# Query loads of a retention-plus-MLP kernel: runs of four tokens, four heads in each half of the partitions

## The chip, the core and the metric

The kernel runs on one core of a Trainium2 chip. A core has TensorE (PE in the profile; PEld is its weight load), VectorE (DVE), ScalarE (ACT), GpSimd (POOL) and SyncE (SP, which here only issues DMAs), 16 DMA engines that they share, an on-chip memory of 128 partitions and PSUM with 8 banks, into which TensorE writes. The metric is the device time of one execution in microseconds; a kernel's time is the median of its runs.

## The reference

Eight batches, eight heads, 576 tokens, head size 64. Retention (scores times a decay that depends on the distance of the tokens, no softmax), then a two-layer MLP with g = h cos(h). All inputs and the output are float32.

```python
scores = scale * np.matmul(q, k.transpose(0, 1, 3, 2))            # q, k, v: (8, 8, 576, 64)
gamma = 1.0 - 2.0 ** (-5.0 - np.arange(H, dtype=np.float32))
Dmat = np.where(rel >= 0, gamma[:, None, None] ** rel[None, :, :], 0.0)   # rel = query pos - key pos
attn = np.matmul(scores * Dmat[None], v)
x = attn.transpose(0, 2, 1, 3).reshape(4608, 512)
h = x @ w_in                                                      # (512, 2048)
out = (h * np.cos(h)) @ w_out                                     # (2048, 512)
```

## The kernel before

**Retention.** Each batch is cut into two units of 256 tokens and a remainder of 64. Since gamma^(i-j) = gamma^i gamma^-j, q is multiplied by a table of gamma^i/8 (WQ) and v by one of gamma^-j (WV) when they are cast to bf16 (line 597: `qnat`, `natv`); k is only cast (`natk`, line 548). Inside a unit the scores are masked with 0 or 1 (`pt`, line 706, tables TR); between stretches of a unit, and between units, a state K'V is carried (`sba`, `sbb`, `sbr`). q and k are transposed to `qt` and `kt`, in the first four units by TensorE (line 621, copied out of PSUM by ScalarE or VectorE), later by DMA transposes (line 636). Scores, states and outputs are 64x64 matmuls, four side by side on the array (line 667). The outputs are copied from PSUM to `xt` as x transposed (lines 547 and 548).

**Coarse and fine.** Six units, those of batches 0 and 1 and the first of batches 2 and 3, are *coarse*: a partition holds two neighbouring tokens of all eight heads, loaded in one DMA of 512 KB in runs of 512 bytes, and stretches have 128 tokens. The other ten are *fine*: a partition holds one token, each half of 128 tokens has its own DMA in runs of 256 bytes, and stretches have 64 tokens. Remainders have one DMA of 128 KB per batch, on the lower or the upper 64 partitions.

**MLP.** Two units, one of each of two batches, form a tile of 512 tokens; there are nine. The first layer of tiles 0 to 3 is direct (lines 871, 880, 883), that of tiles 4 to 8 goes by seven products in place of eight (lines 983 to 1000), as does the second layer of all (line 1140). For tile 0 two quarters of the first layer are done for each batch by itself, so that they can begin when the first unit is through.

**What sets the order.** The kernel is built as a graph of tasks with estimated durations (lines 131 to 364). A planner runs that graph once, with one list of work for each engine, and the order that it gives is written out as the program; `SHIFT` (line 382) is a table of corrections to the tasks' priorities. Each engine then works through its list in that order and waits on semaphores. All loads of q, k and v are issued by SP in one queue, among them the transposes and the stores; the weights (`win`, `wout`) are issued by GpSimd, each behind the landing of certain q or k loads (`SLABS`, line 380). q has two staging buffers (`stgq`). Where the planner sees a gap on TensorE in the first part, it puts in matmuls on a tile of ones (`warm`, line 492); they compute nothing that is used.

The program starts with the loads that wait for nothing, then the constants (line 498 on: iota and affine_select on GpSimd, memsets on VectorE, exp on ScalarE), and then the planned order.

Of the kernel before, what the change touches and what calls it, by code (L numbers as in the profile page):

```python
# [6 lines left out]
ALU = mybir.AluOpType  # L7
AF = mybir.ActivationFunctionType
F32 = mybir.dt.float32
BF16 = mybir.dt.bfloat16  # L10
# [358 lines left out]
class Kernel:  # L369
# [13 lines left out]
        "Iic;6r$0X*%'(rv/|*2|K$-\\.xP)s7VxS/#u$F?$1t%6D&')'Zx%YG1f<&\\T$aB&y6*G5/`r,{w)zf2bt)t5)^Z,n4&w<)v3&r%"  # L383
        "%4c*\\T-a&$t#%ll%h1%ZX)kq'uX%fA$pg+h6%|)$c)8#U%k4%@E'gh(gT&u7({#&,)<q|/w,,wz%b(-v+.o6&mQ2z]'|&3zK&im"
        "'HD$3A&Dx(G@$(M&(+/#U'.$,=b&-()(`&3C&#h&#U(lF$Md/F7((E&>A$#U(|K%F++wd$cl%t6/F|'qh$sM$Rq$\\n&SH(;8'k8"
        "%q$%nx$Cu&p/$o)&vD$I+.+5.lh'X7&do%1a(8`&lN$5F$|K&xt'2Y(:k4lM0ho'|K6{y%42-4WE:n)l,$t@&|K${y(v2*6u,n/"
        "$|K$|K'z5(eg+k8&3,*Y\\%mf*.J8#U.vK,Y@7l`&l6'`,-w<+wQ(o2$|K%wF$-O%v|(/>.j4-i)%dp$om-|K24w&$7)<+*>=%\\V"
        "(HH-jx-iu**H+5a&u,$@V%i3$NR%p7)iR'j8&kV$fS&qI,0-*Pk.WA-:&+a`'6.1rc,)L-hD&ux%KK*U?'1@'Ym&K{'d5&:r%/i"
        "+pa%d^%ap$oN$(T$_G'oQ,CJ$#Y,3t$#U)vZ1|K&=S$)k$/^$3:0n5$xC&^`2%nB86''y&#x%#U=ve'R'&k3%Y2&j1'd8'xH(iL"
        '-8w'  # L390
# [9 lines left out]
    def __init__(self, nc, es, q, k, v, w_in, w_out, out):  # L400
# [10 lines left out]
        self.WV = sb("wv", [128, NT], F32)  # L411
        self.WQ = sb("wq", [128, NT], F32)
        self.IDN = sb("idn", [128, 128], BF16)
        self.TR = {2: sb("tr2", [128, 256], BF16), 1: sb("tr1", [128, 64], BF16)}
        self.TB = {2: sb("tb2", [128, 256], BF16), 1: sb("tb1", [128, 64], BF16)}
# [82 lines left out]
    def constants(self):  # L498
# [4 lines left out]
        for y in range(2):  # L503
# [5 lines left out]
            allow_small_or_imprecise_dtypes=True), w=[("i", 4)])  # L509
        for i, t in enumerate((self.IA, self.IB)):  # L510
            P.add("pool", lambda e, i=i, t=t: e.iota(
                ap(t, NT, 0, 128, 32, [1, 8]), [[0, 8]], base=512 - 64 * i, channel_multiplier=1,
                allow_small_or_imprecise_dtypes=True), w=[("i", 2 + i)])
# [3 lines left out]
        for h in range(H):  # L517
            P.add("dve", lambda e, h=h: e.memset(ap(self.LG, NT, 0, 128, h, [8, NT // 8]), lng[h]), w=[("lg", h)])
        P.add("dve", lambda e: e.memset(self.CPI.ap(), math.pi / 2), w=["cpi"])
        P.add("dve", lambda e: e.tensor_copy(ap(self.IA, NT, 64, 64, 32, [1, 8]), ap(self.IB, NT, 64, 64, 32, [1, 8])),  # L520
# [793 lines left out]
```

## Time and profile before

| | |
|---|---|
| median of 3 runs | 285.07 us (284.45 to 286.09) |
| profiled execution | 284.38 us |
| its span, from the first instruction to the last | 282.6 us |
| busy: PE, DVE, ACT, POOL | 274.2, 224.0, 175.5, 151.8 us |
| granted TensorE clock | 1.0 |
| read from and written to HBM | 36.70 MB and 9.44 MB |
| q loads: 512 KB x6, 256 KB x20, 128 KB x8; median from issue to landing | 7.1, 5.0, 3.4 us |

The page gives totals, a strip of 40 slices of the span (7.07 us each) with the busy share in tenths, the DMA queues, and the costliest groups of instructions. Besides it the trace answers questions: the chain of work that ended last (each step is what released the next), stretches of the span with the busy time of each engine, all instructions in order of time, and for a tile, who waits for it. A line in a group is the line of the kernel that issued it.

### The profile page before, as it was taken

The numbers are of one execution on the slowest core, as the hardware profiler recorded it, in microseconds if no ns is written. First come the engines' busy times: TensorE is split into PE (matmuls) and PEld (weight loads), VectorE is DVE, ScalarE is ACT, GpSimd is POOL, SyncE is SP. The second block draws the span as 40 slices with busy tenths as digits, with TensorE's granted clock in tenths as the row PEclk, the third lists the DMA queues.
The fourth block names the chain that finished last, engine by engine and source line by source line (L and its number), as shares of the span: only waits on it lengthen the run. The fifth ranks groups of instructions, "written<-read, shape, count | busy, mean of one in ns | idle before, by whom it ended". The sixth has DMA issues, their size and how long they took to land.

```text
span 282.6 us, 9717 instructions
## 1 busy us (share of the span) xinstructions
PE 274.2 (97%) x4093; PEld 216.6 (77%) x4093; DVE 224.0 (79%) x387; ACT 175.5 (62%) x357; POOL 151.8 (54%) x170
## 2 busy tenths in 40 slices
PE   7889989999999999999999999999999999999995
PEld 2457577888884667557888888888888888888884
DVE  3587789998757788888778896799769988896762
ACT  5257866372537645763567767895784777787420
POOL 5461942478244625744789659966495161545300
PEclk9999999999999999999999999999999999999999
DMA  7999999999999999999999999997861200400115
GB/s 197 266 224 278 251 186 265 285 208 219 199 229 204 175 235 175 244 178 250 286 170 224 241 206 235 198 201 171 176 77 69 81 6 0 151 0 2 72 41 187
DMA packets 133131, 49.91 MB, mean 177 GB/s; under 512 B 105440, under 2 KB 128992, under 8 KB 133088
## 3 DMA queue, kind: packets, MB, share of 16 engines
q1 hardware_dynamic: 128576, 44.84, 75.0%
q0 software_dynamic: 4224, 4.19, 9.3%
q8 instruction: 32, 0.52, 0.8%
q10 hardware_dynamic: 288, 0.26, 0.3%
q14 instruction: 11, 0.09, 0.1%
HBM read 36.70 MB, written 9.44 MB: 163 GB/s over the span
## 4 chain that ended last, share of the span: by engine, by line
PE 93%; DVE 3%; DMA 1%; ACT 1%; issue 0%; DVEq 0%
PE bk L1140 40%; PE bk L1000 22%; PE bk L871 19%; PE bk L667 10%; DVE pt L706 2%; DMA stgq<-in_q_dram 1%; PE bk L621 1%; PE bk L492 1%; ACT cb L880 1%; DVE gt L883 0%; DVE kt L548 0%; DVE qnat L597 0%; ACT xt L547 0%; ACT natk L547 0%; ACT qt L547 0%
## 5 line engine op out<-in xcount | busy, mean ns | idle before, releaser
L989 POOL TENSOR_TENSOR gt<-sq,cb 128x512 bf16<-128x512 f32 x40 | 45.9, 1161 | 35.5 <-ACT cb L985 13.1
L871 PE MATMUL bk<-xt,win 128*128 128x256 bf16 (+1 forms) x352 | 60.7, 321 | 0.7 <-ACT xt L547 0.5
L880 ACT ACTIVATE cb<-bk 128x256 bf16<-128x256 f32 (+1 forms) x88 | 41.9, 483 | 21.3 <-PE bk L871 19.0
L883 DVE TENSOR_TENSOR gt<-bk,cb 128x256 bf16<-128x256 f32 (+1 forms) x88 | 46.3, 542 | 10.9 <-ACT cb L880 7.9
L597 POOL TENSOR_TENSOR natv<-stgv,wv 128x512 bf16<-128x512 f32 x36 | 37.2, 1042 | 31.6 <-DVE s L1077 8.2
L871 PEld LDWEIGHTS bk<-xt,win 128*128 128x128 bf16 x352 | 33.1, 98 | 20.2 <-ACT xt L547 1.3
L597 POOL TENSOR_TENSOR qnat<-stgq,wq 128x512 bf16<-128x512 f32 x32 | 33.3, 1049 | 27.5 <-DMA stgq<-in_q_dram 8.9
L989 DVE TENSOR_TENSOR gt<-bk,cb 128x512 bf16<-128x512 f32 x40 | 27.1, 687 | 11.5 <-ACT cb L985 10.8
L1140 PE MATMUL bk<-wout,s 128*128 128x256 bf16 x288 | 36.3, 273 | 0.0
L1140 PE MATMUL bk<-tw,s 128*128 128x256 bf16 x288 | 36.2, 273 | 0.0
L1140 PE MATMUL bk<-wout,gt 128*128 128x256 bf16 x288 | 35.7, 273 | 0.0
L1000 PE MATMUL bk<-xt,win 128*128 128x256 bf16 x240 | 34.7, 273 | 0.0
L706 DVE TENSOR_TENSOR pt<-bk,tr 128x512 bf16<-128x512 f32 x48 | 30.6, 683 | 3.0 <-PE bk L667 3.0
L547 ACT ACTIVATE sn<-bk 128x512 f32<-128x512 f32 (+1 forms) x29 | 16.2, 567 | 26.8 <-PE bk L1140 26.7
L983 DVE TENSOR_TENSOR sq<-bk,sq 128x512 f32<-128x512 f32 x40 | 27.0, 685 | 5.8 <-PE bk L1000 4.9
L1140 PEld LDWEIGHTS bk<-tw,s 128*128 128x128 bf16 x288 | 27.6, 98 | 4.1
L1140 PEld LDWEIGHTS bk<-wout,s 128*128 128x128 bf16 x288 | 27.6, 98 | 3.9
L1140 PEld LDWEIGHTS bk<-wout,gt 128*128 128x128 bf16 x288 | 27.9, 98 | 3.5 <-issue 0.2
L985 ACT ACTIVATE cb<-sq 128x512 bf16<-128x512 f32 x40 | 24.9, 629 | 8.7 <-DVE sq L983 7.7
L1129 DVE TENSOR_TENSOR os<-bk,sn 128x512 f32<-128x512 f32 (+1 forms) x28 | 18.6, 668 | 10.8 <-PE bk L1140 10.7
L548 POOL CAST natk<-stgk 128x512 bf16<-128x512 f32 x34 | 20.5, 622 | 9.8 <-PE bk L667 3.9
L985 ACT ACTIVATE cb<-bk 128x512 bf16<-128x512 f32 x40 | 23.5, 597 | 3.7 <-PE bk L1000 2.4
(82 smaller groups left out, 426.2 us busy)
## 6 DMA issues: line engine op xcount, KB each, us to landing
out_dram<-os SPq DMA_DIRECT2D x16, 512.0 KB, 4.1
stgk<-in_k_dram SPq DMA_DIRECT2D x20, 256.0 KB, 5.0
stgq<-in_q_dram SPq DMA_DIRECT2D x20, 256.0 KB, 5.0
stgv<-in_v_dram SPq DMA_DIRECT2D x20, 256.0 KB, 5.1
stgq<-in_q_dram SPq DMA_DIRECT2D x6, 512.0 KB, 7.1
stgk<-in_k_dram SPq DMA_DIRECT2D x6, 512.0 KB, 8.5
stgv<-in_v_dram SPq DMA_DIRECT2D x6, 512.0 KB, 8.1
win<-in_moe_w_in_dram POOLq DMA_DIRECT2D x4, 512.0 KB, 8.4
```

What stands on the lines that cost most here:

```text
L548: return self.one(eng, dur, lambda e: e.tensor_copy(dst(), src()), r=r, w=w, port=eng == "pool", **kw)
L597: self.one(eng, 610 if eng == "dve" else 1030, lambda e, out=out, inp=inp, tab=tab, col=col, hs=hs: e.tensor_tensor(out(), inp(), ap(tab, ...
L667: return lambda e: e.matmul(out(), lhs(), rhs(), start=start, stop=True, skip_group_check=True)
L706: self.one("dve", 610, lambda e, r=r, b=b, pt=pt: e.tensor_tensor(ap(self.at(pt), 1024, 0, 128, 512 * r, [64 * ny * ny, 8 // ny // ny], [1 ...
L871: inst = e.matmul(ap(self.at(bk), 512, 0, 128, 0, [1, n]), ap(self.WIN, 4 * DFF, 0, 128, c * DFF + 128 * f, [1, 128]), ap(self.at(xt), 204 ...
L880: self.one("act", n - 15, lambda e: e.activation(ap(self.at(cb), TB, 0, 128, 0, [1, n]), ap(self.at(bk), 512, 0, 128, 0, [1, n]), AF.Sin, ...
L883: self.one("dve", 75 + n / 0.96, lambda e: e.tensor_tensor(ap(self.at(gt), NF * TB, 0, 128, f * TB + 256 * h0, [1, n]), ap(self.at(bk), 51 ...
L983: self.one("dve", 610, lambda e: e.tensor_tensor(half(src), self.at(bank).ap(), half(src), ALU.add), r=[(bank,)], w=four(src))
L985: self.one("act", 530 if name else 490, lambda e: e.activation(self.at(cb).ap(), ap(self.at(src), size, 0, 128, 0, [1, 512]), AF.Sin, bias ...
L989: self.one(eng, 1120 if name else 610, lambda e: e.tensor_tensor(ap(self.at(gt), NF * TB, 0, 128, (8 * n + 2 * g) * TB + 256 * h, [TB, 2], ...
L1000: inst = e.matmul(ap(self.at(bank), 512, 0, 128, 256 * f, [1, 256]), l(c, f), rr(c), stop=True, skip_group_check=True, start=(first and f ...
L1140: inst = e.matmul(place(bank, tt), l(f, tt), rr(f), stop=True, skip_group_check=True, start=(first and f == 0 and tt < len(bank)))
```

## The change

A unit's q is loaded so that a partition holds four neighbouring tokens of four heads: heads 0 to 3 in partitions 0 to 63, heads 4 to 7 in partitions 64 to 127. That makes runs of 1 KB, and two DMAs of 256 KB for every unit, coarse or fine. The remainders stay as they are, and so do k and v. What follows from it: q has its own decay table (`WQ`, 40 columns: 8 for the remainders, 32 for the units, from the new `IQ` and `LQ`); `WV` goes into the tile `IA`. A block of `qt` then holds one of the four token residues, and `queries` picks the columns for a stretch: four runs of 32 (coarse) or 16 (fine). The masks have the queries in that order (`TR[2]` and the new `TR[4]`), and the copies to `xt` put the tokens back: they write every fourth element. In the graph a q load of a unit is two tasks with an estimate of 725 ns each on the DMA engines (before: 1840 for a coarse unit, 1200 for each half of a fine one). `SHIFT` is a new table.

```diff
--- before.py
+++ after.py
@@ -380,14 +380,13 @@
     SHIFT = (
...
     )
@@ -408,11 +407,12 @@
         self.TX = {n: sb(f"tx{n}", [128, 2048], BF16) for n in (1, 2, 4)}
-        self.WV = sb("wv", [128, NT], F32)
-        self.WQ = sb("wq", [128, NT], F32)
+        self.WQ = sb("wq", [128, 40], F32)
+        self.LQ = sb("lq", [128, 32], F32)
+        self.IQ = sb("iq", [128, 32], F32)
         self.IDN = sb("idn", [128, 128], BF16)
-        self.TR = {2: sb("tr2", [128, 256], BF16), 1: sb("tr1", [128, 64], BF16)}
-        self.TB = {2: sb("tb2", [128, 256], BF16), 1: sb("tb1", [128, 64], BF16)}
+        self.TR = {2: sb("tr2", [128, 256], BF16), 1: sb("tr1", [128, 64], BF16), 4: sb("tr4", [128, 64], BF16)}
+        self.TB = {2: sb("tb2", [128, 256], BF16), 1: sb("tb1", [128, 64], BF16), 4: sb("tb4", [128, 64], BF16)}
         self.ONE = sb("one", [128, 128], BF16)
@@ -507,6 +507,10 @@
             allow_small_or_imprecise_dtypes=True), w=[("i", 4)])
+        for i, t in enumerate((self.IQ, self.LQ)):
+            P.add("pool", lambda e, i=i, t=t: e.iota(
+                ap(t, 32, 0, 128, 0, [16, 2], [4, 4], [1, 4]), [[256, 2], [1, 4], [0, 4]], base=-256 * i, channel_multiplier=4,
+                allow_small_or_imprecise_dtypes=True), w=[("iq", i)])
         for i, t in enumerate((self.IA, self.IB)):
@@ -517,26 +521,35 @@
         P.add("dve", lambda e: e.memset(self.CPI.ap(), math.pi / 2), w=["cpi"])
+        P.add("dve", lambda e: e.tensor_copy(ap(self.IQ, 32, 64, 64, 0, [1, 32]), ap(self.LQ, 32, 64, 64, 0, [1, 32])),
+              r=[("iq", 1)], w=[("iq", 0)])
+        for h in range(H):
+            P.add("dve", lambda e, h=h: e.memset(ap(self.LQ, 32, 64 * (h // 4), 64, h % 4, [4, 8]), lng[h]),
+                  r=[("iq", 0)], w=[("iq", 1)] if h == 0 else [("lq", h)])
+        P.add("dve", lambda e: e.tensor_tensor(self.LQ.ap(), self.IQ.ap(), self.LQ.ap(), ALU.mult),
+              r=[("iq", 0), ("iq", 1)] + [("lq", h) for h in range(1, H)], w=["lqx"])
         P.add("dve", lambda e: e.tensor_copy(ap(self.IA, NT, 64, 64, 32, [1, 8]), ap(self.IB, NT, 64, 64, 32, [1, 8])),
...
               r=[("i", n) for n in (0, 1, 2, 4)] + [("lg", h) for h in range(H)], w=["lgx"])
-        P.add("act", lambda e: e.activation(self.WQ.ap(), self.LG.ap(), AF.Exp, bias=math.log(1.0 / 8.0), scale=1.0),
-              r=["lgx"], w=["wq"])
-        P.add("act", lambda e: e.activation(self.WV.ap(), self.LG.ap(), AF.Exp, scale=-1.0), r=["lgx"], w=["wv"])
+        P.add("act", lambda e: e.activation(ap(self.WQ, 40, 0, 128, 8, [1, 32]), self.LQ.ap(), AF.Exp, bias=math.log(1.0 / 8.0), scale=1.0),
+              r=["lqx"], w=["wq"])
+        P.add("act", lambda e: e.activation(ap(self.WQ, 40, 0, 128, 0, [1, 8]), ap(self.LG, NT, 0, 128, 32, [1, 8]), AF.Exp,
+                                            bias=math.log(1.0 / 8.0), scale=1.0), r=["lgx", "wq"], w=["wr"])
+        P.add("act", lambda e: e.activation(self.IA.ap(), self.LG.ap(), AF.Exp, scale=-1.0), r=["lgx"], w=["wv"])
         P.add("act", lambda e: e.activation(ap(self.IB, NT, 0, 128, 0, [1, 1]), self.CPI.ap(), AF.Sin), r=["cpi"], w=[("i", 3)])
-        for ny in (2, 1):
+        for kind, ny, run in ((2, 2, 32), (4, 1, 16), (1, 1, 64)):
             n = 64 * ny * ny
-            for dst, up, name in ((self.TR[ny], 0, "tr"), (self.TB[ny], 1, "tb")):
+            for dst, up, name in ((self.TR[kind], 0, "tr"), (self.TB[kind], 1, "tb")):
                 for y in range(ny):
-                    dims = ([64, 2], [1, 64]) if ny == 2 else ([1, 64],)
-                    P.add("pool", lambda e, dst=dst, up=up, ny=ny, y=y, n=n, dims=dims: e.affine_select(
+                    dims = ([1, 64],) if kind == 1 else ([run, 4], [1, run])
+                    P.add("pool", lambda e, dst=dst, up=up, kind=kind, ny=ny, run=run, y=y, n=n, dims=dims: e.affine_select(
                         ap(dst, n, 0, 128, 128 * y, *dims), ap(self.ONE, 128, 0, 128, 0, *dims),
-                        pattern=[[1, 2], [2, 64]] if ny == 2 else [[1, 64]], compare_op=ALU.is_ge, fill=0.0,
-                        base=64 * ny * up - y, channel_multiplier=-ny), r=["one"], w=[(name, ny, y)])
-            P.add("dve", lambda e, ny=ny, n=n: e.tensor_copy(
-                ap(self.TR[ny], n, 64, 64, 0, [1, n]), ap(self.TB[ny], n, 64, 64, 0, [1, n])),
-                r=[("tb", ny, y) for y in range(ny)], w=[("tr", ny, y) for y in range(ny)])
+                        pattern=[[1, 64]] if kind == 1 else [[1, 4], [4, run]], compare_op=ALU.is_ge, fill=0.0,
+                        base=64 * ny * up - y, channel_multiplier=-ny), r=["one"], w=[(name, kind, y)])
+            P.add("dve", lambda e, kind=kind, n=n: e.tensor_copy(
+                ap(self.TR[kind], n, 64, 64, 0, [1, n]), ap(self.TB[kind], n, 64, 64, 0, [1, n])),
+                r=[("tb", kind, y) for y in range(ny)], w=[("tr", kind, y) for y in range(ny)])
 
@@ -552,6 +565,14 @@
         src = self.src["qkv".index(which)]
+        if which == "q" and u[1] < 2:
+            for i in range(2):
+                at = (u[0] * H * S + 4 * S * i + 256 * u[1]) * D
+                self.one("sp", 500, lambda e, i=i, at=at: e.dma_start(
+                    ap(self.at(stg), 1024, 64 * i, 64, 0, [256, 4], [1, 256]),
+                    bass.AP(src, at, [[4 * D, 64], [S * D, 4], [1, 4 * D]])),
+                    r=gate, w=[(stg, i), (stg, i + 2)], sem=lambda i=i: f"{which}{stg.slot}_{i}", dma=725, tail=720 if fast else 1800)
+            return stg
         for i, (p0, n, o, ny, b, r0) in enumerate(rows):
@@ -575,10 +596,17 @@
             for y in range(2):
-                rs = [(stg, i) for i in ((2 * y, 2 * y + 1) if fine else range(4))]
+                four = which == "q" and not rem
+                rs = [(stg, i) for i in ((2 * y, 2 * y + 1) if fine and not four else range(4))]
 
...
                     return ap(self.at(nb), 1024, 0, 128, 512 * y, [256, 2], [64, 4], [1, D])
+
+                def out4(y=y, nb=nb):
+                    return ap(self.at(nb), 1024, 0, 128, 512 * y, [128, 4], [64, 2], [1, D])
+
+                def inp4(y=y, stg=stg):
+                    return ap(self.at(stg), 1024, 0, 128, 256 * y, [64, 4], [512, 2], [1, D])
 
@@ -590,12 +618,17 @@
                 else:
-                    tab, key = (self.WV, "wv") if which == "v" else (self.WQ, "wq")
+                    tab, key = (self.IA, "wv") if which == "v" else (self.WQ, "wr" if rem else "wq")
                     col = 32 if rem else 40 * fine + 16 * u[1] + 8 * y
+                    if four:
+                        out, inp, hs, col = out4, inp4, [[4, 4], [2, 2]], 8 + 16 * u[1] + y
+                    elif which == "q":
+                        col = 0
+                    nt = 40 if which == "q" else NT
                     eng = "dve" if fast and which == "q" else self.CASTS.get(u, "pp pp pp")[(3 if which == "q" else 6) + y]
                     eng = {"d": "dve", "p": "pool"}.get(eng, eng)
-                    self.one(eng, 610 if eng == "dve" else 1030, lambda e, out=out, inp=inp, tab=tab, col=col, hs=hs: e.tensor_tensor(
-                        out(), inp(), ap(tab, NT, 0, 128, col, *hs, [0, D]), ALU.mult),
+                    self.one(eng, 610 if eng == "dve" else 1030, lambda e, out=out, inp=inp, tab=tab, col=col, hs=hs, nt=nt: e.tensor_tensor(
+                        out(), inp(), ap(tab, nt, 0, 128, col, *hs, [0, D]), ALU.mult),
                         r=rs + [(key,)], w=[(nb, y)], port=eng == "pool")
@@ -666,11 +699,18 @@
 
+    def queries(self, u, qt, r, s, c, y):
+        if u[1] == 2:
+            return ap(self.at(qt), 1024, 64 * r, 64, c * 128 + 64 * s + 512 * y, [1, 64])
+        n = 16 if self.fine(u) else 32
+        return ap(self.at(qt), 1024, 64 * r, 64, 512 * (c // 2) + 64 * (c % 2) + n * (2 * y + s if n == 16 else s), [128, 4], [1, n])
+
     def scores(self, u, prio, todo, split, extra=(), join=None):
...
         N, ny = (64, 1) if rem else (128, 2)
+        kind = 4 if self.fine(u) else ny
         phases = []
@@ -681,9 +721,7 @@
                         def rhs(r=r, s=s, c=c, y=y):
-                            o = c * 128 + 64 * s
-                            return ap(self.at(qt), 1024, 64 * r, 64, o + 512 * y, [1, 64]) if rem else ap(
-                                self.at(qt), 1024, 64 * r, 64, o, [512, 2], [1, 64])
+                            return self.queries(u, qt, r, s, c, y)
                         lanes[r, s].append((N, self.mm(
@@ -706,8 +744,8 @@
                 ap(self.at(b), 512, 0, 128, 0, [64 * ny * ny, 8 // ny // ny], [1, 64 * ny * ny]),
-                ap(self.TR[ny], 64 * ny * ny, 0, 128, 0, [0, 8 // ny // ny], [1, 64 * ny * ny]), ALU.mult),
-                r=[(b,)] + [("tr", ny, y) for y in range(ny)], w=[(pt, r)])
+                ap(self.TR[kind], 64 * ny * ny, 0, 128, 0, [0, 8 // ny // ny], [1, 64 * ny * ny]), ALU.mult),
+                r=[(b,)] + [("tr", kind, y) for y in range(ny)], w=[(pt, r)])
         for v, s in todo:
@@ -771,7 +809,7 @@
                     main[s, p].append((N, self.mm(
-                        lambda c=c, y=y: ap(self.at(ob[s]), 512, 64 * p, 64, ((y * 4 if rem else 0) + c) * N, [1, N]),
+                        lambda c=c, y=y: ap(self.at(ob[s]), 512, 64 * p, 64, (2 * c + y if fine else y * 4 + c if rem else c) * N, [1, N]),
                         lambda c=c, y=y: ap(self.at(nv), 1024, 64 * s, 64, 512 * y + (2 * c + p) * D, [1, D]),
@@ -791,11 +829,9 @@
                     def rhs(i=i, y=y):
-                        o = i * 128 + 64 * s
-                        return ap(self.at(qt), 1024, 64 * r, 64, o + 512 * y, [1, 64]) if rem else ap(
-                            self.at(qt), 1024, 64 * r, 64, o, [512, 2], [1, 64])
+                        return self.queries(u, qt, r, s, i, y)
                     to[r, p].append((N, self.mm(
-                        lambda c=c, y=y: ap(self.at(ob[s]), 512, 64 * p, 64, (y * 4 + c) * N, [1, N]),
+                        lambda c=c, y=y: ap(self.at(ob[s]), 512, 64 * p, 64, (2 * c + y if fine else y * 4 + c) * N, [1, N]),
                         lambda i=i, src=src: ap(self.at(src), 256, 64 * r, 64, i * 64, [1, 64]),
@@ -814,13 +850,15 @@
             for s in range(2):
-                if rem:
-                    o, d = (64 * s, 1) if fine else (s, 2)
-                    dst = lambda o=o, d=d: ap(self.at(xt), 2048, 0, 128, 1024 * half + o, [128, 2], [256, 4], [d, 64])
+                if fine:
+                    dst = lambda s=s: ap(self.at(xt), 2048, 0, 128, 1024 * half + 64 * s, [128, 8], [1, 4], [4, 16])
+                    src = lambda s=s: ap(self.at(ob[s]), 512, 0, 128, 0, [64, 8], [16, 4], [1, 16])
+                elif rem:
+                    dst = lambda s=s: ap(self.at(xt), 2048, 0, 128, 1024 * half + s, [128, 2], [256, 4], [2, 64])
                     src = lambda s=s: ap(self.at(ob[s]), 512, 0, 128, 0, [256, 2], [64, 4], [1, 64])
                 else:
-                    dst = lambda s=s: ap(self.at(xt), 2048, 0, 128, 1024 * half + 128 * s, [256, 4], [1, 2], [2, 64])
-                    src = lambda s=s: ap(self.at(ob[s]), 512, 0, 128, 0, [128, 4], [64, 2], [1, 64])
+                    dst = lambda s=s: ap(self.at(xt), 2048, 0, 128, 1024 * half + 128 * s, [256, 4], [1, 4], [4, 32])
+                    src = lambda s=s: ap(self.at(ob[s]), 512, 0, 128, 0, [128, 4], [32, 4], [1, 32])
                 self.copy("dve" if s and (rem or u in self.SWIFT) else "act", 590, dst, src, [(ob[s],)], [(xt, half, s)])
```

More of the change, by code (lines that the diff above doesn't have):

```diff
@@ L382 @@
     SHIFT = (
[L383 to L390, printed above, removed]
+        "##h%5Q)#fBk*&|K%r7%n(X3f$^A'qx$``+J'$5/?d=/XJ,wv)vt&lJ)z/)v4&#U$&U$<($Fb$Co&#U$I99ys,#U2g^)+z)[%&|K"
+        "2_o8$=%%7$A{)zD+Cw'm\\.Gj%H$%Wx+_;&j{)no(8f&B,$K*$u/&hm$mX$%-4|K&m'&w0$mp(|C'n+'w|&\\y.{F4_g5l8)#U&?#"
+        "&9x%e)$uJ%xZ%r$%q#%k]$t4%rk%v\\%o4)ix&t/'x{4ky1{:^t,&rT&s&&tf.<5)wF&mq&zg%iI8:8+sZ,dH'Hk0:'%IU(6T*#d"
+        "'cC)x=%4W%yT%Sx$eJ'ek'8E*%v')s,497+.*?E:2A'#b%*{$km)(#+kf7r.$6Y%wy)t%$m>&{n)r:(*c(sh-Sf*z{1zL*t-@xt"
+        "%9?2?[({y&xi&s&)t(+cQ0xI$\\@4dU'%t)vd+`uG1S.-l,[x'x>%|K$nu'jz5|&)qN$sZ%zy${((qn$#U&pz*uu'oH2|K(WQ$vQ"
+        ")xL%|G${N.)['5k%cB&{[2?i&<u)?f;3S&ji4|K(k')rq&q:&o2&r>&tz&p[$wg'ec0s,.k_%t>$133S<'w?.+80&N*$j)8{$Ij"
+        "(6@+[h%XX5{]'{+&dp%|K&z#<l]0p|,Yj"
     )
```

## The prediction

> **What bounds the kernel now.** I read the page's totals and slices first, then the table of stretches, then the chain of waits, then the rates of the loads.
>
> ```profile
> PE 274.2 (97%) x4093; PEld 216.6 (77%) x4093; DVE 224.0 (79%) x387; ACT 175.5 (62%) x357; POOL 151.8 (54%) x170
> ...
> PE   7889989999999999999999999999999999999995
> ...
> DMA  7999999999999999999999999997861200400115
> ...
> q1 hardware_dynamic: 128576, 44.84, 75.0%
> ```
>
> TensorE is busy all the time but for the first six slices and the last; the DMA engines are full as well, up to slice 28. Two full resources mean that the DMA time matters only where TensorE waits for it. The stretches say where (length, then PE busy with its instructions, clock, DMA share, GB/s; in the second table filler alone, line 492, matmuls on a tile of ones that the program puts in gaps):
>
> ```profile
> 0.00:50.00 50.00, 44.86 (x608) 1.00 1.11 239
> 50.00:265.00 215.00, 214.84 (x3359) 1.00 0.84 167
> 265.00:282.60 17.60, 14.50 (x133) 1.00 0.34 121
> ```
>
> ```profile
> 0.00:50.00 50.00, 10.36 (x28) 2.82 (x28) 1.00 1.11 239
> 50.00:265.00 215.00, 0.00 (x0) 0.00 (x0) 1.00 0.84 167
> ```
>
> In the first 50 us TensorE idles 50.00 - 44.86 = 5.1 us and fills 10.4 us: 15.5 us lost. From 50 to 265 us it loses 0.16 us in all. So a faster load earns something in the first 50 us alone; a slower one can cost anywhere. The chain of waits shows the start (start, length, what):
>
> ```profile
> 0.81 4.12 DMA stgq<-in_q_dram
> 5.03 0.70 DVE qnat L597
> 5.78 1.21 PE bk L621 x8
> 6.99 0.85 PE bk L492 x2
> 7.84 0.87 PE bk L621 x8
> 8.73 0.44 DVE kt L548
> 9.30 0.66 PE bk L667 x14
> 9.99 2.50 DVE pt L706 x4
> ```
>
> q is the first load; k lies behind it in the same queue (VectorE and GpSimd turn it to bf16 from 6.81 us), and the scores at 9.30 need both. Last the rates at which loads run, from stretches filled with one kind:
>
> ```profile
> 3.50:5.00 1.50, 1.50 (x4) 0.30 (x2) 0.00 (x0) 0.53 (x2) 0.00 (x0) 1.00 1.17 326
> 79.00:83.00 4.00, 4.00 (x93) 3.43 (x91) 2.08 (x4) 1.18 (x3) 0.56 (x1) 1.00 1.19 228
> 178.00:182.00 4.00, 4.00 (x54) 3.36 (x55) 2.71 (x5) 3.40 (x8) 4.00 (x6) 1.00 0.82 187
> 190.00:192.00 2.00, 2.00 (x63) 1.80 (x63) 2.00 (x5) 1.69 (x5) 1.13 (x2) 1.00 0.83 192
> ```
>
> The first is the first q (512-byte runs, 128 partitions): 326 GB/s. The second is loads in 256-byte runs over 128 partitions: 228. The last two are the loads of the 64-token remainders: 256-byte runs again, but each DMA writes 64 partitions only, alternately the lower and the upper half: 187 and 192 GB/s, with the DMA share at 0.82 where the others show 1.17 to 1.19.
>
> **The change part by part.** The sum is made against the profiled execution, 284.38 us (span 282.6 and 1.8 around it); the median of the runs shown, 285.07, is 0.69 above it.
>
> *The q loads.* Every unit of 256 tokens gets two DMAs of 256 KB, each on one half of the partitions in 1 KB runs. For six units (the coarse ones) that replaces one DMA in 512-byte runs, for ten (fine) two DMAs in 256-byte runs. No row has 1 KB runs into 64 partitions. Lower bound: the trace's records of 1 KB packets (stores at the end, all 128 partitions) have 46 to 48 ns each, so 512 x 47 / 16 = 1.50 us for a unit. Upper bound: the 64-partition rows, 524 KB / 187 GB/s = 2.80 us. A coarse unit takes 524 / 326 = 1.61 us now, a fine one 524 / 228 = 2.30. So coarse goes from 1.61 to between 1.50 and 2.80, fine from 2.30 to the same. I take 2.76 (190 GB/s): the remainder loads are nearest, being HBM loads into the same alternating halves, and the stores share only the run length.
> The row leaves open why halves are slower, a fixed cost of each DMA or the half itself, and only the first would shrink with longer runs. [...]
>
> *First unit.* q complete moves from 4.93 us by 2.76 - 1.61 = +1.15; k, v and all that hangs on them with it. Bounds -0.11 and +1.19. SP issues one DMA more ahead of k and v (0.46 us): k's packets cannot start before q's are through, so it costs nothing; if that cover went, 0.46.
>
> *Second unit.* Its q adds another 1.15, so k lands 2.3 late; now it lands at about 14.86 (GpSimd's next weight DMA waits for it there). Its casts run at 15.59 and 16.41 and its transposes at 17.26, so about 0.9 of the 2.3 is slack: 1.4 late at the scores (18.78), and at the second half of the first tile (24.00). TensorE's only other work there is eight first-half groups, and the filler shows that they do not suffice. Delay by then: +1.4 (bounds -0.1 and +2.3).
>
> *Units three and four* (scores at 35.40 and 49.96). Their loads wait behind the weight slabs, but TensorE has solid MLP work from 24.0 to 35.4, moved by the same 1.4. A further 1.15 per load eats into that cover: I take +0.3 (bounds -0.5 and +1.2).
>
> *Two later coarse and ten fine units.* 2 x 1.15 + 10 x 0.46 = +6.9 us of DMA time at most likely, -0.2 - 8.0 = -8.2 at best. Cost nothing: after 50 us TensorE waits 0.16 us in 215. If the cover goes, see the fourth rival. SP issues six DMAs more in all, at 0.4 to 0.8 us; where its queue stands behind a buffer wait, k, v and the transposes behind it move too, which belongs to that rival.
>
> *Readers of q.* Both q multiplies of a fine unit now wait for both DMAs, where each waited for its own: at most one DMA later, 1.4 us on GpSimd (54% busy), hidden. The multiplies keep 128x512 (1047 ns). GpSimd's first weight DMA waits for the first q DMA only, so it can go out earlier (bounds: a 1.2 us gain for that slab; or the slab in front of k). Taken as zero.
>
> *Constants.* GpSimd: two iotas (0.14 to 0.18) and two selects (0.23); its list ends at 3.1 and its next work is at 5.24. VectorE: eight memsets, two copies and a multiply, some 0.9 us. ScalarE: one more exp, 0.25, before the table load that ends at 3.83. The q table is ready at about 3.2 in place of 2.36, q lands at 4.93: cover 1.7 us. Cost 0; uncovered 0.9.
>
> *Output copies.* Contiguous copies to xt take 591 to 603 ns on ScalarE, those with every second element 733 to 747. Now all write every fourth. Fine ones: from 597 to between 740 and 885 (twice the step), ten on each of ScalarE and VectorE, 1.4 to 2.9 us on an engine at 62%: hidden. Coarse: 0 to +0.15, twice on the start's path: +0.1.
>
> *Matmuls.* Scores and state reads take q columns in four runs of 32 or 16 where they had two of 64 or one. A group of 32 scores with two runs takes 0.64 us and one of 32 on contiguous pt also 0.64, so runs of 64 are free. Shorter runs: 0 by that row; if a column in short runs cost double, some 600 fine matmuls, four side by side, by 27 ns, is 4 us (fifth case). Masks have the same shape.
>
> *The order.* Which instruction stands where cannot be read from the table of shifts. Zero, with -2.0 (the stall named below) and +3 as bounds.
>
> Sum: 1.4 + 0.3 + 0.1 = +1.8: 284.38 + 1.8 = 286.2 in a profile, 285.07 + 1.8 = **286.9** as a median.
>
> **The rivals.**
> *Faster: the halves run at full rate and the new order uses it.* Place: the third unit. Its q, issued at 19.68, lands at 26.86 (GpSimd idles 7.6 us for it), scores wait until 35.40 and outputs until 38.41; between 30 and 40 us TensorE loses 0.84 idle and 1.20 filler. If q and what follows are there 2 us sooner, all 2.0 are saved; 0.1 to 0.3 more at the start: 285.07 - 2.2 = 282.9. For it: the loss is real, and 1 KB packets elsewhere do run at 47 ns. Against it: a coarse unit saves 0.11 us by that row, and the 0.8 that a fine unit saves falls where TensorE does not wait. It decides from a unit in under 1.6 us.
> *Hidden.* Halves between 1.6 and 2.0 us, start later by under 0.5, the order makes it up: 285.1. For it: if only a fixed cost per DMA explains the 0.82 share, 1 KB runs dilute it.
> *TensorE starves later.* DMA is full up to 205 us; 6.9 us more of it, and an order laid out for quick q loads, make scores wait in tiles 2 to 7, say half of 6.9: 286.9 + 3.4 = 290.3 if none is caught up, 288.5 if half is. Against it: 0.16 us of waits today.
> *Short runs slow the matmuls:* 285.07 + 4 = 289.1. Against it: 64-column runs are free.
> *The change does not do what it says*, few packets with no shorter load, is my forecast itself.
>
> **How the numbers follow.** Under 0.5% (1.4 us) this kernel's runs, 284.45 to 286.09, can't be told from no change. Forecast 0.42 (own range 285.9 to 288.0; a quarter of it inside the 0.5%), faster 0.25, hidden 0.16, starving 0.12, short runs 0.05. Faster by over 0.5%: 0.25. Within: 0.16 + 0.42/4 = 0.26. Slower: 0.49. The range leaves out about a third of the faster case below 282.9 and the dearer half of the last two above 288.8: 282.9 to 288.8.
>
> **What would show it.** q complete at about 6.1 in the chain (4.9 or less: the rate was wrong); 187 to 220 GB/s in the stretch of the first q against 326; scores of the first unit at 10.4 in place of 9.30; the second half of tile 0 at about 25.4; from 50 to 265 us PE still idle under 0.5 us; ScalarE copies to xt all at 740 or more; groups of 48 fine scores still 0.51 us. Wrong if halves are not slower, or if the new order moves filler out of the first 50 us by more than 1.8 us.

## The result and the profile after

The changed kernel takes 297.6 us (median of 6 runs, 296.95 to 298.94); the kernel before took 285.97 beside it. The ratio is 1.0416, with a 95% interval from 1.0379 to 1.0454: slower by 4.2%. The forecast was 286.9 with a range up to 288.8: the right side, and far too small. The profiled execution took 298.94 us, the longest of its six. Medians and ratios below leave out a run that lies more than 1.5% above the fastest of its kernel (one each in two experiments).

The page of the changed kernel, totals, strip and load queue:

```profile
span 297.1 us, 9745 instructions
...
PE 276.7 (93%) x4089; PEld 215.5 (73%) x4089; DVE 241.0 (81%) x398; ACT 186.4 (63%) x358; POOL 157.2 (53%) x174
...
PE   5988999999799989978999999999999999999996
...
q1 hardware_dynamic: 110240, 44.84, 72.3%
```

The queue moves the same 44.84 MB in 110240 packets in place of 128576, and their time is 72.3% of a longer span, 215 us in place of 212: fewer packets, no shorter loads. TensorE's strip has holes in the middle now. The stretches of the changed kernel (length, PE, PEld, DVE, ACT, POOL busy with their instructions, clock, DMA share, GB/s):

```profile
0.00:50.00 50.00, 42.56 (x581) 27.46 (x581) 35.02 (x86) 30.88 (x64) 25.00 (x46) 0.93 1.09 212
50.00:265.00 215.00, 204.93 (x3247) 162.56 (x3245) 183.28 (x280) 141.39 (x267) 123.46 (x121) 1.00 0.85 173
```

In the first 50 us TensorE idles 7.4 us and fills 9.3, 16.7 us where 15.5 were lost before: 1.2 more, near the +1.4 of the forecast. From 50 to 265 us it idles 10.1 us where it idled 0.16. That is most of the loss: 9.9 of the 14.5 us by which the profiled span is longer, and it lies where the forecast had put nothing. Another 2.5 us is time in which TensorE is busy, 276.7 us against 274.2. What TensorE waited for in the changed kernel (total, times, longest, all in us):

```profile
PE bk L909 <- ACT xt L560: 2.8, 5, 0.8
PE bk L700 <- issue: 2.6, 2, 1.7
PE bk L654 <- ACT natk L560: 2.6, 1, 2.6
PE bk L700 <- DMA qt<-qnat: 1.6, 1, 1.6
PE bk L700 <- POOL natk L561: 1.5, 1, 1.5
```

Two kinds stand side by side: the copies to xt (4.7 us with four smaller rows that are not shown) and data that come late out of loads, casts and transposes. (`issue` means that the profile shows nothing waited for.) The copies themselves, before and after (the first two rows are of the kernel before, the last two of the changed one; ns shortest, median, longest):

```profile
L547 ACT ACTIVATE xt<-bk x21: 589/733/752, 13.9 to 230.9; 128x512 bf16<-128x512 f32 x21
L548 DVE CAST xt<-bk x15: 678/692/742, 13.8 to 231.7; 128x512 bf16<-128x512 f32 x15
```

```profile
L560 ACT ACTIVATE xt<-bk x21: 729/1309/1418, 15.5 to 245.7; 128x512 bf16<-128x512 f32 x21
L561 DVE CAST xt<-bk x15: 730/1293/1302, 15.3 to 245.6; 128x512 bf16<-128x512 f32 x15
```

They take about twice the time; the forecast had 740 to 885. The start of the changed kernel, in order of time:

```profile
7.00 0.63 ACT L560 ACTIVATE natk<-stgk 128x512 bf16<-128x512 f32 x1 [1.86 <-DMA stgk<-in_k_dram]
7.69 1.03 PE L654 MATMUL bk<-idn,natk 128*128 128x128 bf16 x8 [2.60 <-ACT natk L560]
8.06 1.29 DVE L630 TENSOR_TENSOR qnat<-stgq,wq 128x512 bf16<-128x512 f32 x2 [3.93 <-DMA stgq<-in_q_dram]
10.63 1.07 PE L700 MATMUL bk<-qt,kt 64*64 64x128 bf16 x32 [0.18 <-DVE qt L561]
```

The new order issues half of q, then k, then the other half of q: k is cast first, the second half of q is there at 8.06 (the whole of q at 5.03 before; times of the multiply that reads it). The first scores stand at 10.63 against 9.30; the forecast had 10.4.

### The profile page after: what moved, and what is told of

It reads as the page before. It is cut to its first block, busy times and chain, and to the rows that moved or that the text cites. A ratio compares the mean times of both kernels' runs of the same rounds, so it can differ in the third digit from the quotient of the medians.

```text
span 297.1 us, 9745 instructions
## 1 busy us (share of the span) xinstructions
PE 276.7 (93%) x4089; PEld 215.5 (73%) x4089; DVE 241.0 (81%) x398; ACT 186.4 (63%) x358; POOL 157.2 (53%) x174
## 3 DMA queue, kind: packets, MB, share of 16 engines
q1 hardware_dynamic: 110240, 44.84, 72.3%
## 4 chain that ended last, share of the span: by engine, by line
PE 73%; DMA 6%; DVE 5%; ACT 5%; SPq 5%; issue 3%; POOL 2%; DVEq 0%; POOLq 0%
PE bk L1178 32%; PE bk L1038 20%; PE bk L909 13%; PE bk L700 7%; DMA stgv<-in_v_dram 5%; ACT xt L560 3%; SPq L579 2%; DVE xt L561 2%; SPq L571 2%; DVE gt L921 1%; SPq L669 1%; DMA qt<-qnat 1%; POOL tx L945 1%; POOL natv L630 1%; PE bk L654 1%
## 5 line engine op out<-in xcount | busy, mean ns | idle before, releaser
L1027 POOL TENSOR_TENSOR gt<-sq,cb 128x512 bf16<-128x512 f32 x40 | 46.7, 1169 | 43.4 <-ACT cb L1023 17.1
L921 DVE TENSOR_TENSOR gt<-bk,cb 128x256 bf16<-128x256 f32 (+1 forms) x88 | 45.5, 541 | 13.6 <-ACT cb L918 11.7
L630 POOL TENSOR_TENSOR natv<-stgv,ia 128x512 bf16<-128x512 f32 x36 | 39.2, 1097 | 21.4 <-DMA stgv<-in_v_dram 11.3
L561 POOL CAST natk<-stgk 128x512 bf16<-128x512 f32 x34 | 21.6, 642 | 37.4 <-DMA stgk<-in_k_dram 33.9
L630 POOL TENSOR_TENSOR qnat<-stgq,wq 128x512 bf16<-128x512 f32 x32 | 34.5, 1090 | 12.6 <-DMA stgq<-in_q_dram 4.5
L1178 PE MATMUL bk<-wout,gt 128*128 128x256 bf16 x288 | 36.6, 273 | 1.1 <-ACT xt L560 0.6
## 6 DMA issues: line engine op xcount, KB each, us to landing
stgv<-in_v_dram SPq DMA_DIRECT2D x6, 512.0 KB, 10.1
```

The lines of the kernel that those rows point to most:

```text
L561: return self.one(eng, dur, lambda e: e.tensor_copy(dst(), src()), r=r, w=w, port=eng == "pool", **kw)
L630: self.one(eng, 610 if eng == "dve" else 1030, lambda e, out=out, inp=inp, tab=tab, col=col, hs=hs, nt=nt: e.tensor_tensor(out(), inp(), a ...
L921: self.one("dve", 75 + n / 0.96, lambda e: e.tensor_tensor(ap(self.at(gt), NF * TB, 0, 128, f * TB + 256 * h0, [1, n]), ap(self.at(bk), 51 ...
L1027: self.one(eng, 1120 if name else 610, lambda e: e.tensor_tensor(ap(self.at(gt), NF * TB, 0, 128, (8 * n + 2 * g) * TB + 256 * h, [TB, 2], ...
L1178: inst = e.matmul(place(bank, tt), l(f, tt), rr(f), stop=True, skip_group_check=True, start=(first and f == 0 and tt < len(bank)))
```

## The experiments

Three theories were set against each other: **L**, the q loads are slower; **C**, the copies to xt are slower and hold up TensorE; **O**, the new order is worse. Ratios are to the kernel before in the same call, with 95% intervals. Kernels in the order of before have the same instructions in the same places as it, but for the edit.

**1. One part alone, in the order of before.** The loads; with them both q multiplies of a fine unit wait for both of its DMAs, as in the changed kernel:

```diff
-ap(self.at(stg), 1024, p0, n, o, [w, H], [1, w]), bass.AP(src, at, [[w, n], [S * D, H], [1, w]])
+ap(self.at(stg), 1024, 64 * i, 64, 0, [256, 4], [1, 256]), bass.AP(src, at, [[4 * D, 64], [S * D, 4], [1, 4 * D]])   # i = 0, 1
```

> The kernel before, order and copies untouched, with q loaded as the changed kernel loads it, two DMAs of 64 partitions in 1 KB runs (the multiply reads the staging tile as before, so heads and tokens are mixed up: a time of the loads alone). Theory L as recorded: q complete about 1.15 us later at the start, 287 to 288.5. Rival, the loads run at the full rate of 1 KB packets (46 ns): 285 to 286. Theory C and O leave it between these two.

Measured: 294.0 us, ratio 1.030 (1.0248 to 1.0352). Theory L, well above the range given, and five times the recorded size (8.9 us against 1.8). The copies (destinations only):

```diff
-dst: [256, 4], [1, 2], [2, 64]      # coarse; fine: [128, 2], [256, 4], [1, 64]
+dst: [256, 4], [1, 4], [4, 32]      # coarse; fine: [128, 8], [1, 4], [4, 16]
```

> The kernel before, order and loads untouched, with the copies to xt writing every fourth element as the changed kernel does (the tokens in xt are then in a wrong order; nothing else changes). Theory C: 286 rises to 292 to 297, TensorE idles at the matmuls that read xt after 50 us. Theories L and O: 286 to 288, since ScalarE is busy 62% of the span and VectorE 79%.

Measured: 290.9, ratio 1.0214 (1.0152 to 1.0277), a little under the range of theory C and well over what the other two allowed. TensorE's longest wait in that kernel:

```profile
PE bk L873 <- ACT xt L547: 3.4, 5, 1.0
```

Both together:

> The kernel before, its order untouched, with both the q loads in halves and the copies to every fourth element. If loads (8.9 alone) and copies (5.8 alone) add up: 299.5 to 300.5. If they hide behind each other: 294 to 297. Against the changed kernel (297.6) it says what the new order is worth under the new loads and copies.

Measured: 297.5, ratio 1.0394 (1.0338 to 1.045). 3.0% and 2.1% alone make 3.9% together, so a good fifth of the two hides behind each other; the time lies between the two expectations. The order of before with the new loads and copies is as slow as the changed kernel (1.0416; the intervals overlap): under them the new order, with its constants, masks and q columns, neither loses nor gains anything that these runs can tell.

**How late loads cost nine microseconds.** In the loads-alone kernel the first q multiply starts at 5.57 in place of 5.03. That is not yet the loss: the scores of the second unit start at 18.98 in place of 18.78. The delay grows along a chain that was not in the forecast: k of the fourth unit releases the weight DMAs (GpSimd, line 855 of before) at 35.5 in place of 32.4; their landing releases the loads of the next units (SP, 44.1 in place of 41.9); and SP issues the transposes of those units 4.4 and 5.5 us late (before first, loads alone second; the next ones are at 67.56 and 73.02):

```profile
55.90 2.98 SPq L636 DMA_TRANSPOSE kt<-natk  x1
```

```profile
60.31 4.15 SPq L653 DMA_TRANSPOSE kt<-natk  x1
```

TensorE, working through a fixed order, then stands (PE alone, of the kernel before and of the loads alone):

```profile
50.00:100.00 50.00, 50.00 (x835) 1.00 1.10 217
```

```profile
50.00:100.00 50.00, 44.57 (x674) 0.97 1.13 213
```

5.4 us idle in that stretch; from 100 to 265 us both are busy. The idle time is three waits: 0.91 us at 51.56 for a weight slab, 1.12 at 79.27 for VectorE, and 3.40 at 94.86 for v on GpSimd. The longest, in the loads-alone kernel:

```profile
92.76 1.05 POOL L614 TENSOR_TENSOR qnat<-stgq,wq 128x512 bf16<-128x512 f32 x1 [5.78 <-DMA stgq<-in_q_dram]
93.76 1.04 POOL L614 TENSOR_TENSOR natv<-stgv,wv 128x512 bf16<-128x512 f32 x1
...
94.86 0.32 PE L684 MATMUL bk<-natv,natk 64*64 64x64 bf16 x16 [3.40 <-POOL natv L614]
```

and the same multiply in the kernel before:

```profile
83.02 1.05 POOL L597 TENSOR_TENSOR qnat<-stgq,wq 128x512 bf16<-128x512 f32 x1
```

It is the first of the two q multiplies of a fine unit. Before, it waits for its own DMA alone, which landed at 81.89. Here it waits for both: the unit's first DMA landed at 86.88, the second, issued at 87.12 (82.96 before), at 92.69; and v stands behind it on GpSimd. No run has the halves without this wait.

Of the 9.3 us by which this span is longer, 5.5 are idle time after 50 us and 1.1 before. In the other 2.7 TensorE is busy with the same instructions: in the 5 us after the long wait its granted clock was 0.66, and the 160 first-layer matmuls of 512 columns took 38.6 us in place of 36.9. The first layer's work that fills the gaps later is not free to be moved forward, since the order is written out.

**2. What is slow in the loads.** Same order, same two DMAs of 256 KB in 1 KB runs, over all 128 partitions:

```diff
-ap(self.at(stg), 1024, 64 * i, 64, 0, [256, 4], [1, 256])
+ap(self.at(stg), 1024, 0, 128, 512 * i, [256, 2], [1, 256])
```

> As the kernel before with the q loads in halves (that one took 294.0 against 285.1), same order, same two DMAs of 256 KB in 1 KB runs, but each writes all 128 partitions (two runs in each; the bytes come from other places of q, so this is a time of the loads alone). Theory H (a DMA into 64 partitions is slow, by ports or in another way): the loss goes, 284.5 to 286.5. Rival S (two DMAs in place of one, later completion and the second multiply's wait cost it, whatever the partitions): 291 to 294.

Measured: 285.6, ratio 1.002 (0.9984 to 1.0057): the whole loss is gone, though the multiplies wait for both DMAs here too (the one above for 3.34 us, and TensorE behind it for 0.96). The halves with the old run lengths:

```diff
-ap(self.at(stg), 1024, 64 * i, 64, 0, [256, 4], [1, 256])
+ap(self.at(stg), 1024, 64 * i, 64, 0, [w, n], [1, w])    # fine: w = 64, n = 16; coarse: w = 128, n = 8
```

> The same with DMAs of 64 partitions and the old run lengths (512 and 256 bytes; bytes again from other places of q): the halves without the longer runs. Theory H: 293 or more, and at least as slow as with 1 KB runs. Rival R (1 KB runs are themselves slow into this staging tile, or collide with the 512-byte runs of k and v): 285 to 288.

Measured: 297.9, ratio 1.0439 (1.0347 to 1.053). So it is the halves; longer runs seem to soften it, but the interval just touches that of the loads alone. The queue of the two kernels with 1 KB runs, halves first:

```profile
q1 hardware_dynamic: 110240, 44.84, 75.2%
```

```profile
q1 hardware_dynamic: 110240, 44.84, 67.5%
```

The same packets, and 7.7 points less of the engines' time when they go to all partitions. In the packet records the 1 KB loads have 44 ns at the shortest in both, and a mean of 68 in halves against 55; the 512-byte packets of k and v, which did not change, have 36 against 29.

**3. Undoing parts in the changed kernel.** Copies in the old form, with the new loads and order:

```diff
-dst: [128, 8], [1, 4], [4, 16]; src: [64, 8], [16, 4], [1, 16]     # fine
+dst: [128, 8], [1, 64]; src: [64, 8], [1, 64]
```

> The changed kernel, with the copies to xt writing as the kernel before does (fine: contiguous, coarse: every second element); the tokens in xt are then in another order, so this leaves out the part of the computation that puts them back. Instruction order and loads stay as in the changed kernel. Theory C (the copies carry the loss: they take 1.29 to 1.31 us in place of 0.59 to 0.75, and lie between outputs and MLP): 297.6 falls to 287 to 290. Theory L (the slower q loads carry it, as my prediction had it): 296 to 297.5. Theory O (the new order carries it): 295 to 297.5. Copies to xt should show 590 to 750 ns on both engines.

Measured: 295.9, ratio 1.0378 (1.0326 to 1.0431). Theory C alone falls here: 1.7 us of 11.6, and the intervals of the two ratios overlap. Loads in the old form, with the slow copies:

```diff
-ap(self.at(stg), 1024, 64 * i, 64, 0, [256, 4], [1, 256])
+ap(self.at(stg), 1024, 0, 128, 512 * i, [w, hs], [1, w])     # fine: w = 64, hs = 8; coarse: w = 128, hs = 4
```

> The changed kernel with only the q loads in the old form (two DMAs over 128 partitions for every unit; bytes land in other places, a time of the loads alone), copies to every fourth element. If the loads carry most, as they do in the order of before (8.9 of the 14.7 that the two single changes add up to), 297.6 falls to 289 to 292; with the copies alone it fell only to 295.9.

Measured: 293.5, ratio 1.0301 (1.0229 to 1.0372); a little over the range given. Both in the old form:

> The changed kernel with both old forms, q loaded over all partitions in 512 and 256-byte runs and the copies to xt as before (token order left wrong): what is left is the new order, the constants and the short runs of q columns. If loads and copies explain the loss, 285 to 288; if the order itself costs, 290 or more.

Measured: 288.1, ratio 1.0107 (1.005 to 1.0164). Alone they give back 1.7 and 4.1 us, together 9.5: while the loads are late, quick copies give back little, and the other way round. What is left, 1.1%, lies between the two expectations and was open here.

**4. Other places to put the tokens back.** Here TensorE reads the q columns in token order, each column 256 bytes from the one before, and the copies are contiguous:

```diff
-512 * (c // 2) + 64 * (c % 2) + n * ..., [128, 4], [1, n]
+512 * (c // 2) + 64 * (c % 2) + n * ..., [1, n], [128, 4]
```

> The changed kernel with the tokens put back at another place: scores and state reads take the q columns in token order (32 or 16 steps of four columns that lie 128 apart), masks in token order, copies to xt contiguous for coarse and fine units. Loads and instruction order as in the changed kernel; all of the computation is done. Theory C: 285 to 289, if TensorE reads columns 256 bytes apart at full speed; if each such column costs double, 4 to 8 us more, and the groups of fine scores take over 0.6 us in place of 0.51. Theories L and O: 296 or more.

Measured: 310.2, ratio 1.0869 (1.0817 to 1.0922), above every range given. Its groups of matmuls, scores of 128 columns and of 64 (after the first bar: busy us, mean ns of one):

```profile
L700 PE MATMUL bk<-qt,kt 64*64 64x128 bf16 x192 | 12.2, 391 | 0.4 <-ACT kt L560 0.3 <-DVE qt L561 0.2
...
L700 PE MATMUL bk<-qt,kt 64*64 64x64 bf16 x384 | 11.3, 269 | 0.0
```

In the kernels before and after they have 235 and 195. Scores of 128 columns take 156 ns more, 1.2 ns a column. The runs of 32 and 16 of the changed kernel cost nothing. This place is worse than the copies.

How a copy's time depends on its pattern was measured by itself, in one run:

> The kernel before, and after its last work forty more copies on ScalarE and forty on VectorE, of 128x512 from PSUM to a tile of bf16, four each of ten patterns: write step 1, 2, 3 and 4 elements; the coarse pattern of before; the two patterns of the changed kernel; runs of 16 that are contiguous but lie apart; and the two patterns of the changed kernel turned round, so that PSUM is read in steps and the tile is written contiguously. Theory W (the write step makes them slow): step 2 as the coarse pattern, 0.73 to 0.75; step 4 and both patterns of the changed kernel 1.2 to 1.3; runs of 16 and the turned ones 0.6 to 0.7. Rival R (short runs make them slow): contiguous runs of 16 are slow too, plain step 4 is not. Rival P (PSUM read in steps is as dear): the turned ones 1.0 or more.

Measured, one row for each of write steps 1, 2, 3 and 4, for the changed kernel's two patterns, and for the first of these turned round (the other has the same 597; ScalarE, ns shortest, median, longest):

```profile
L456 ACT ACTIVATE xt<-bk x4: 592/597/597, 278.6 to 305.9; 128x512 bf16<-128x512 f32 x4
L457 ACT ACTIVATE xt<-bk x4: 737/737/739, 279.2 to 306.5; 128x512 bf16<-128x512 f32 x4
L458 ACT ACTIVATE xt<-bk x4: 1019/1019/1019, 280.0 to 307.3; 128x512 bf16<-128x512 f32 x4
L459 ACT ACTIVATE xt<-bk x4: 1302/1302/1302, 281.1 to 308.3; 128x512 bf16<-128x512 f32 x4
...
L461 ACT ACTIVATE xt<-bk x4: 1301/1301/1302, 283.2 to 310.4; 128x512 bf16<-128x512 f32 x4
L462 ACT ACTIVATE xt<-bk x4: 1292/1292/1292, 284.5 to 311.8; 128x512 bf16<-128x512 f32 x4
...
L464 ACT ACTIVATE xt<-bk x4: 597/597/597, 286.4 to 313.7; 128x512 bf16<-128x512 f32 x4
```

Theory W in full: among these patterns the write step alone sets it, 0.28 us for each element of step from 2 on; contiguous runs of 16 that lie apart take 597, and reading PSUM in steps of 16 or 32 takes 597 too. VectorE does the same: 691, 726, 1008, 1290, and 691 turned round. So the copies can be had for nothing:

```diff
-dst: [128, 8], [1, 4], [4, 16]; src: [64, 8], [16, 4], [1, 16]
+dst: [128, 8], [4, 16], [1, 4]; src: [64, 8], [1, 16], [16, 4]
```

> The changed kernel with the tokens put back by reading PSUM in steps of 16 or 32 and writing xt contiguously; loads and order as in the changed kernel, all of the computation done. Theory W: as with the old copies, 295 to 296.5, copies at 0.6 to 0.7. Rival P: 297 or more.

Measured: 296.5, ratio 1.0386 (1.0344 to 1.0429), copies on ScalarE at a median of 592. As with the old copies: not worth more while the loads are late.

**5. Is the order bad, or only its assumptions?** Loads in 1 KB runs over all partitions and turned copies, in the order of the changed kernel:

> The changed kernel, order untouched, with q in 1 KB runs over all 128 partitions (two DMAs of 256 KB; bytes from other places of q, so a time alone) and the copies to xt reading PSUM in steps and writing contiguously: loads and copies as fast as the planner took them to be. If the new order is good once its assumptions hold: 281 to 285. If the order, the constants or the short runs cost by themselves, as the 288.1 with both old forms suggests: 287 to 289.

Measured: 283.6, ratio 0.9915 (0.9884 to 0.9945). With quick loads and copies (planned with 725 ns for each half, where the packet records give 53 ns x 256 / 16 = 0.85 us, and 590 for a copy) this order loses nothing; the kernel even beats the one before. How much of that is the order's is open: the turned copies alone give 0.55% in the order of before (below). The 1.1% that was left with both old forms goes when loads and coarse copies are quick; which of the two it is was not tried. This kernel leaves the right placing of q out, so it is no version to use. The turned copies in the kernel before:

> The kernel before with only the coarse copies to xt turned round, PSUM read in steps of 64, xt written contiguously: 0.60 in place of 0.74 on ScalarE. All of the computation is done. TensorE waits for such a copy 0.5 us in all, so 284 to 285.5: at most 0.5 us better than the kernel before.

Measured: 285.0, ratio 0.9945 (0.9913 to 0.9978), with the whole computation done: half a percent better than the kernel before, and the only complete version that was.

Last, four heads in the even and four in the odd partitions, with the whole computation and turned copies:

```diff
-ap(self.at(stg), 1024, 64 * i, 64, 0, [256, 4], [1, 256])
+bass.AP(self.at(stg), 1024 * i, [[2048, 64], [256, 4], [1, 256]])
...
-512 * (c // 2) + 64 * (c % 2) + n * ..., [128, 4], [1, n]
+512 * (c // 2) + c % 2 + 2 * n * ..., [128, 4], [2, n]
```

> The changed kernel with four heads in the even and four in the odd partitions in place of lower and upper half: each of the two DMAs still writes 64 partitions in 1 KB runs, but every second of all 128; the decay table is built for that, TensorE takes every second column of qt, and the copies read PSUM in steps. All of the computation is done, order as in the changed kernel. Theory H-place (where the 64 partitions lie makes the halves slow): 283 to 285.5, near the 283.6 of the kernel with 1 KB runs over all partitions. Rival H-number (64 partitions in one DMA are slow wherever they lie): 295 to 297, as the changed kernel with turned copies (296.5). If every second column costs TensorE time as columns 128 apart did, 2 to 4 us more.

Measured: 285.9, ratio 1.0007 (0.9981 to 1.0033), 0.4 above the range for place and 9 below that for number. The same number of DMAs, partitions and runs as in the kernel with turned copies (296.5), only in other partitions, but for the q table and the columns that go with it: 10.6 us. The 1 KB packets of q have a mean of 54 ns, against 72 there. So it is where the 64 partitions lie, not how many they are; why the place matters, no run shows. Scores on every second column keep their times (233 and 195 ns). Why this kernel stays 2.3 us above the 283.6 is not settled; its first casts of k and q start 0.3 and 0.45 us later, and its granted clock fell to 0.79 between 5 and 10 us where the other kept 1.00.

## Why the prediction was wrong

**The bound on the q loads: direction right, size too large.** Halves are slow (294.0 us, against 285.6 with as many DMAs and the same runs over all partitions), and it is the half itself, not a fixed cost of each DMA. But 2.76 us for a unit was too much: by the packet records of the loads-alone kernel, 68 ns x 512 / 16 = 2.2 us, and the stretch from 3.5 to 5.0 us moved 231 GB/s, some of it k and v, where 187 to 220 were expected. The first q multiply is 0.54 us late there (5.57 against 5.03) and 1.06 late (6.09) in the kernel with loads and copies, whose q loads are the same; +1.15 was taken.

**k at the start: right size, other cause.** Its first cast on GpSimd is 0.7 late (7.51 against 6.81). But it is as late (7.62) in the full-width kernel of section 2, where the first q multiply starts at 4.44. So "k's packets cannot start before q's are through", which no row had shown, does not hold: in the loads alone the first 512-byte packet (k or v) starts at 4.09, and q lands at 5.44; in the changed kernel the first starts at 3.36, and the last 1 KB packet of the half of q that was issued ahead of k ends at 3.96. With one more DMA ahead of it k was issued 0.5 to 1.0 us later; whether that is the cause was not tried.

**"Cost nothing: after 50 us TensorE waits 0.16 us in 215."** This is the step that failed. An idle time near zero was read as slack, although the forecast itself says that a slower load can cost anywhere. It says that the order just fits; nothing in it says how late a load may be. The loads alone made TensorE idle 5.65 us from 50 to 265 us, nearly all of it between 50 and 100, through the chain from k to weights to the next loads. The rival "TensorE starves later" had the right place, at 288.5 to 290.3 and a chance of 0.12; measured were 294.0 for it alone.

**The readers of q: called hidden, and not hidden.** In the order of before, the wait of a fine unit's first q multiply for the second DMA lies ahead of TensorE's longest idle time (3.40 us). With full-width loads it still cost 0.96 us of TensorE's time, but nothing that the median shows. It was weighed as one multiply that comes later; it holds up all that GpSimd has behind it.

**The output copies: mis-sized, and wrongly called hidden.** The bound "twice the step" went from step 1 to 2 (+144 ns) to step 4 by doubling the increment, 885; the time went to 1.29 to 1.31 us, since each element of step from 2 on took 0.28 us (737, 1019 and 1302 ns in the probe). And the share of ScalarE (62%) says nothing of a copy that stands between the outputs of a unit and the first layer that reads them: +0.1 was taken, the copies alone cost 2.1%.

**The order: zero taken, none seen** under the new loads and copies (1.0416 against 1.0394 in the order of before). Under quick loads and copies the kernel is 0.85% better than before; the order's own share of that is not told apart.

**What held.** The runs of 32 and 16 cost nothing (235 and 195 ns, as before), and the q table is ready at 2.87 (3.2) and hidden. The first scores at 10.63 (10.4) and the loss in the first 50 us of 1.2 (1.4) came out close partly by luck. The order puts half of q behind k (its multiply at 8.06, where 6.1 was named), and 1.2 us of the waits in that stretch (0.80 and 0.38) are for the slow copies to xt, taken at 0.1. In the loads alone the first scores stand at 9.84, and those of the second unit are 0.2 late where 1.4 was forecast.

## What to carry to other kernels

An idle time near zero in a written-out order (0.16 us in 215 here, where late loads then cost 8.9) does not say how late a load may be: cost a slower load along the chain of what its landing releases, the work queued behind its reader included, and not by the waits of the trace before. Spread each DMA over all partitions (285.6 us here, against 294.0 in halves), or over every second one (285.9 against 296.5), not over one half. When a layout must be undone, write contiguously and step through PSUM on the reading side (597 ns a copy on ScalarE, against 1302 with a write step of 4).

## What the runs showed of the hardware

- Copies from PSUM to bf16 in SBUF: write steps of 1, 2, 3 and 4 elements take 597, 737, 1019 and 1302 ns on ScalarE and 691, 726, 1008 and 1290 on VectorE for 128x512; reading PSUM in steps of 16 or 32 elements costs nothing (597 and 691).
- The 64x64 matmuls take every second column (195 and 233 ns for 64 and 128 columns) and runs of 16 or 32 (195 and 235) in the time of whole runs (195 and 235); columns 256 bytes apart cost 1.2 ns more each in the scores (269 and 391).
- Two DMAs of 64 partitions in 1 KB runs: lower and upper half 296.5 us, even and odd 285.9, all else equal but for the table and columns that go with it.
- After TensorE's 2.60 us wait at 5.1 us in the changed kernel its granted clock was 0.75 between 5 and 10 us and 0.57 between 10 and 15, where the kernel before kept 1.00. In the loads alone it was 0.66 from 95 to 100 us, after the wait of 3.40 that ended at 94.86. What this cost was not tried by itself.
